# A gated attention-and-MLP block: score maxima of the first eight head pairs from key chunk differences, with a relu on ScalarE

## The chip, the cores and the metric

The kernel runs on one core of one Trainium2 chip. The metric is the device time of one execution in microseconds (us). The kernel before takes 1845.5 us, the median of three runs (1843.69 to 1846.99). Engines are named as the profile names them: PE (TensorE matmul), PEld (its weight load), DVE (VectorE), ACT (ScalarE), POOL (GpSimd), SP (SyncE, here only a DMA queue).

## The reference

Input x has S = 2048 rows and D = 640 columns; there are H = 32 heads of DH = 20 columns, and the token MLP has a hidden width of 1728. All is float32.

```
def _A_ref(x, wqkv, wo):
    qkv = (x @ wqkv).reshape(B, S, 3, H, Dh).transpose(2, 0, 3, 1, 4)
    q, k, v = qkv[0], qkv[1], qkv[2]
    scores = jnp.einsum("bhqd,bhkd->bhqk", q, k) * (Dh ** -0.5)
    p = softmax(scores, axis=-1)
    o = jnp.einsum("bhqk,bhkd->bhqd", p, v)
    return o.transpose(0, 2, 1, 3).reshape(B, S, D) @ wo

def _B_ref(x, w1, b1, w2, b2):
    h = layernorm(x, axis=-1)
    u = gelu(jnp.einsum("bsd,sf->bdf", h, w1) + b1)
    y = jnp.einsum("bdf,fs->bds", u, w2) + b2
    return y.transpose(0, 2, 1)

g = sigmoid((x * gate_w).sum(-1, keepdims=True))
return g * _A_ref(x, ...) + (1 - g) * _B_ref(x, ...)
```

## The kernel before

Float32 operands are split into a high and a low part (`hi_lo`: the high part by ACT or POOL, the difference by DVE or POOL), and a product is three matmuls. The work has four stages, one after the other on PE.

1. **Projections.** `qk_unit(m, w, q)` makes a 128x512 block of q (m below 5) or k (m from 5 on) in 15 matmuls; ACT writes the high part `evh`, DVE the low part `evl`, and SP stores both to `q_d` or `k_d`. `evh` and `evl` have two buffers each. Four quarters of x (`xh`, `xl`) are split by ACT and DVE as they arrive, between the first units. The v products and the layer norm's sums come between the second and the third block of q and k.
2. **The MLP** (`mlp`), a generator of 2592 steps; one step is a pair of 64-row matmuls of 320 columns (`pair64`). It has two column halves d; each makes 14 tiles u (48 steps, tail tile 32) and 16 tiles y (40 steps). ACT copies finished tiles out (`u_evac`, `y_evac`), POOL adds their two halves, ACT does the gelu and splits weights (`w_split`), POOL makes the weights' low parts. What must happen some steps later is put in the list `soon` with a countdown.
3. **The attention loop**: 16 head pairs, 32 iterations each, 512 in all. An iteration makes four transposed score tiles (`st`), ACT takes exp of each (`pt`), and PE multiplies the previous iteration's four exp tiles with v (`pv`).
4. **The output projection**, gate and store.

Softmax needs the row maxima ahead of the exp. They are made by a second stream of score tiles `s`, the generator `s_stream`: 16 pairs x 2 halves of the queries x 8 query tiles x 4 key chunks of 512 x 2 heads, 2048 tiles. Each is one PE matmul on 60 rows and one DVE `tensor_reduce` (L180) of 128x512 scores in PSUM to one column of `mx`. The two heads of a pair lie in PE's rows 0 to 63 and 64 to 127, so two neighbouring tiles of different heads run side by side. When a half is done, `s_max` and `s_store` reduce further, split and store to `m_d`, from which `load_m` puts the maxima into the extra rows of the q stack that `st` uses.

`s_next` takes the next tile of the stream. `S_AHEAD` = 736 tiles are taken in the MLP, two at a time and evenly over its steps; the other 1312 are taken in the loop, 2 or 3 in each of the first 484 iterations and none in the last 28. Where an engine's order is written by hand (all five engines, each from some point on) it is the order of the code. PSUM has eight banks: four for `st` and the MLP's tiles, three for `s`, one for `pv`. In the loop the third `st` of an iteration with two `s` tiles takes one of the `s` banks. The stacked operands of a pair, `ks` and `qs`, are loaded by 18 DMAs (`load_stack`); during the MLP they wait in the list `drip`, from which SP takes one every four `s` tiles.

Of the kernel before, what the change touches and what calls it, by code (L numbers as in the profile page):

```python
# [13 lines left out]
P = 128  # L14
# [5 lines left out]
FT = 14  # L20
TL = F - FF * P
# [7 lines left out]
def gated_mix(ctx, tc, xT, x, wqk, wv0, wv1, wo, w1, w1t, b1, w2, b2, out):  # L29
# [26 lines left out]
    k_d = dram.tile([2, D, S], F32, name="k_d")  # L56
    m_d = dram.tile([NP, 2, P, 32], F32, name="m_d")
# [13 lines left out]
    def s_tile(shape, name):  # L71
        return psum.tile(shape, F32, tag="s", bufs=3, name=name)
# [67 lines left out]
    def s_max(p, half, mx):  # L140
        mm = cp.tile([P, 16], F32, tag="mm", bufs=2, name=f"mm{p}_{half}")
        mc = cp.tile([P, 32], F32R, tag="mc", bufs=2, name=f"mc{p}_{half}")
        nc.vector.tensor_reduce(mm, mx.rearrange("p k j t -> p (j t) k"), axis=AX.X, op=OP.max)
# [24 lines left out]
    def s_tiles(p):  # L168
        for half in range(2):
            mx = cp.tile([P, 4, 2, 8], F32, tag="mx", bufs=2, name=f"mx{p}_{half}")  # L170
            for t in range(8):
                for kc in range(4):
                    for j in (1, 0):
                        def f(j=j, kc=kc, t=t):
                            ks, qs = s_src[p]
                            ps = s_tile([P, 512], f"s{p}_{half}_{t}_{j}_{kc}")
                            r = slice(64 * j, 64 * j + 3 * DH)
                            nc.tensor.matmul(ps, qs[half][r, t * P:(t + 1) * P], ks[r, kc * 512:(kc + 1) * 512],  # L178
                                             start=True, stop=True)
                            nc.vector.tensor_reduce(mx[:, kc, j, t: t + 1], ps, axis=AX.X, op=OP.max)  # L180
                        yield f
            s_close.append([2, lambda p=p, half=half, mx=mx: s_max(p, half, mx)])

    def s_stream(on_start):
        for p in range(NP):
            on_start(p)
            yield from s_tiles(p)
# [23 lines left out]
    accs = iter(range(1000))  # L211

    def qk_unit(m, w, q):
# [5 lines left out]
        hi_lo(hi, lo, ps, hi_eng=nc.scalar)  # L219
        dst = q_d if m < NC else k_d  # L220
# [3 lines left out]
        nc.sync.dma_start(dst[1, rows, cols], lo.bitcast(F32))  # L224

# [176 lines left out]
    for n, (m, q) in enumerate(units):  # L402
        if q == 0 and n + 4 < len(units):
            w[units[n + 4][0]] = load_w(units[n + 4][0])
        if n == 17:
            s_src[0] = base_stack(0, False, nc.gpsimd)
# [9 lines left out]
        qk_unit(m, w[m], q)  # L416
        if n in (18, 19):
            w_split(n - 18)
# [8 lines left out]

    soon = []
# [9 lines left out]
    def u_evac(f, d, ps, gh, gl):  # L438
# [4 lines left out]
        if f == FF:  # L443
            soon.append([7, lambda: u_swap(d, xg)])
            soon.append([30, lambda: nc.gpsimd.tensor_add(xg, xg, sws.pop())])
            soon.append([44, lambda: u_tail(f, d, xg, gh)])
        else:
            soon.append([18, lambda: u_gelu(f, xg, gh, gl)])
# [89 lines left out]
    S_AHEAD = 736  # L538
    STEPS = 2 * ((FT - 1) * 48 + 32 + NT * 40)

    def start_ahead(p):
        if 2 <= p + 1 < 6:
            s_src[p + 1] = base_stack(p + 1, False, None)
# [4 lines left out]
    for n, _ in enumerate(steps):  # L548
        settle()
        while done + 2 <= S_AHEAD and done < S_AHEAD * (n + 1) / STEPS:  # L550
# [7 lines left out]
            if drip and done % 4 == 0:  # L558
                drip.pop(0)()
# [27 lines left out]
    s_src[6] = s_stack(6)  # L587
# [83 lines left out]
    LEFT = NP * 128 - S_AHEAD  # L671
    for p in range(NP):
# [3 lines left out]
        for it in range(32):  # L676
# [121 lines left out]
```

## Time and profile before

| stage | us from the span's start | length | PE matmuls | ACT busy | DVE busy | POOL busy |
|---|---|---|---|---|---|---|
| projections | 0 to 225.3 | 225.3 | | | | |
| MLP with 736 maximum tiles | 225.3 to 698.5 | 473.2 | 5956 | 226.95 | 466.38 | 382.77 |
| loop, iterations with maximum tiles | 699.5 to 1707.5 | 1008.0 | 7112 | 987.11 | 852.42 | 181.26 |
| loop, last 28 iterations | 1707.5 to 1762.5 | 55.0 | 338 | 55.00 | 5.62 | 11.89 |
| output projection | 1762.5 to 1844.8 | 82.3 | | | | |

The span of the profiled execution is 1844.8 us, 0.7 us under the median of the runs (1845.5). No other time of that execution is given, and sums are made against 1844.8. Busy time is the time in which at least one instruction of the engine ran; PE's is no measure of its load, since its matmuls overlap and their ends are modelled. The granted clock of PE is 0.996 on average. The stages' bounds are the first and last matmuls and exps of the trace.

### The profile page before, as it was taken

To read this page: it belongs to the slowest core of one execution; us is meant where nothing else is said; L and a number is where in the kernel's file an instruction comes from. 1 tells how busy PE (TensorE), PEld (TensorE's weight loads), DVE (VectorE), ACT (ScalarE), POOL (GpSimd) and SP (SyncE) were. 2 spreads that over 40 slices of the span, in tenths; PEclk is the share of its full clock that TensorE was granted. 3 is DMA by queue.
4 is the path that set the end of the run, shared out by engine and by line. 5 is a ranking of instruction groups with operands and counts; after the bars stand their busy time and mean duration, and the time that the engine had idled before them with its cause. 6 is when DMAs were issued, how large, how long until landed. Compare 5 with 4: busy or idle time off the path is not lost. (4 is left out here: it accounts for less than half of the span.)

```text
span 1844.8 us, 39129 instructions
## 1 busy us (share of the span) xinstructions
PE 1829.7 (99%) x14978; PEld 1135.2 (62%) x14978; DVE 1428.9 (77%) x2341; ACT 1361.6 (74%) x2688; POOL 637.1 (35%) x900
## 2 busy tenths in 40 slices
PE   9999999999999999999999999999999999999998
PEld 7998799999999994333333333333333333333378
DVE  4202299999999998888888888888888888888137
ACT  4243244465444448999999999999999999999930
POOL 1013478888887770112112111121321211212210
PEclk9999999999999999999999999999999999999999
DMA  8456766566645645504032324213540423301463
GB/s 289 143 169 212 222 173 173 158 194 193 168 139 166 189 136 121 118 15 103 20 85 61 73 42 93 57 50 78 107 103 24 109 47 77 71 14 23 131 219 132
DMA packets 152831, 216.61 MB, mean 117 GB/s; under 512 B 65698, under 2 KB 92082, under 8 KB 148738
## 3 DMA queue, kind: packets, MB, share of 16 engines
q1 hardware_dynamic: 129172, 178.68, 35.4%
q0 software_dynamic: 14688, 20.78, 5.2%
q10 hardware_dynamic: 8784, 14.65, 2.4%
q8 instruction: 118, 1.93, 0.4%
q14 instruction: 69, 0.57, 0.1%
HBM read 165.43 MB, written 48.25 MB: 116 GB/s over the span
## 5 line engine op out<-in xcount | busy, mean ns | idle before, releaser
L180 DVE TENSOR_REDUCE mx<-s 128x1 f32<-128x512 f32 x2048 | 1293.7, 684 | 159.9 <-PE s L178 119.7
L703 ACT ACTIVATE p<-st 128x512 f32<-128x512 f32 x2048 | 1042.1, 615 | 20.9 <-PE s L178 2.2
L700 PEld LDWEIGHTS st<-qs_True,ks_True 62*128 62x128 f32 x2048 | 307.3, 185 | 485.1 <-ACT p L703 312.9
L700 PE MATMUL st<-qs_True,ks_True 62*128 62x512 f32 x2048 | 579.6, 425 | 0.2 <-ACT ty L477 0.2
L637 PE MATMUL pv<-p,v 128*32 128x512 f32 x4096 | 555.5, 605 | 0.2
L178 PE MATMUL s<-sk,sq 60*128 60x512 f32 x1280 | 423.1, 434 | 0.0
L41 POOL TENSOR_TENSOR wl<-wr,wh 128x512 fp32r<-128x512 f32 x228 | 273.6, 1216 | 59.8 <-ACT wh L38 30.9
L624 POOL DMA_DIRECT2D o_d<-oev x128 | 67.0, 524 | 494.3 <-DVE oev L618 491.6
L178 PE MATMUL s<-ks_False,qs_False 60*128 60x512 f32 x768 | 225.1, 397 | 0.4 <-DVE mx L180 0.3
L46 PE MATMUL y<-gh,wh 64*128 64x320 f32 x896 | 216.8, 308 | 0.0
L46 PE MATMUL y<-gl,wh 64*128 64x320 f32 x832 | 210.3, 306 | 0.0
L46 PE MATMUL y<-gh,wl 64*128 64x320 f32 x832 | 209.4, 305 | 0.0
L38 ACT ACTIVATE wh<-wr 128x512 fp32r<-128x512 f32 (+2 forms) x246 | 135.9, 594 | 90.2 <-PE s L178 29.0
L178 PEld LDWEIGHTS s<-sk,sq 60*128 60x128 f32 x1280 | 197.7, 185 | 1.2
L637 PEld LDWEIGHTS pv<-p,v 128*32 128x32 f32 x4096 | 84.9, 108 | 171.4 <-issue 156.4
L46 PE MATMUL u<-hl,wh 64*128 64x320 f32 x864 | 167.1, 306 | 0.0
L46 PE MATMUL u<-hh,wh 64*128 64x320 f32 x864 | 167.1, 306 | 0.0
L46 PE MATMUL u<-hh,wl 64*128 64x320 f32 x800 | 156.9, 306 | 0.4 <-POOL wl L41 0.4
L46 PEld LDWEIGHTS y<-gh,wh 64*128 64x128 f32 x896 | 155.3, 184 | 0.4
L46 PEld LDWEIGHTS y<-gh,wl 64*128 64x128 f32 x832 | 147.0, 184 | 0.3
L46 PEld LDWEIGHTS y<-gl,wh 64*128 64x128 f32 x832 | 146.9, 184 | 0.0
L178 PEld LDWEIGHTS s<-ks_False,qs_False 60*128 60x128 f32 x768 | 124.4, 184 | 1.1 <-DVE mx L180 1.1
(124 smaller groups left out, 1817.6 us busy)
## 6 DMA issues: line engine op xcount, KB each, us to landing
wr<-in_w_dram SPq DMA_DIRECT2D x196, 256.0 KB
ks_True<-k_d SPq DMA_DIRECT2D x96, 160.0 KB
qs_True<-q_d SPq DMA_DIRECT2D x192, 80.0 KB
sk<-k_d SPq DMA_DIRECT2D x60, 160.0 KB
sq<-q_d SPq DMA_DIRECT2D x120, 80.0 KB
v_d<-vt SPq DMA_DIRECT2D x32, 168.0 KB
v<-v_d SPq DMA_DIRECT2D x16, 336.0 KB
xr<-in_xT_dram SPq DMA_DIRECT2D x20, 256.0 KB
```

The costliest lines, as they stand in the source:

```text
L38: nc.scalar.activation(hi, src, AF.Copy)
L41: (lo_eng or nc.vector).tensor_sub(lo, src, hi.bitcast(F32))
L46: nc.tensor.matmul(ps[k], a[r], b[r], start=start, stop=stop)
L178: nc.tensor.matmul(ps, qs[half][r, t * P:(t + 1) * P], ks[r, kc * 512:(kc + 1) * 512], start=True, stop=True)
L180: nc.vector.tensor_reduce(mx[:, kc, j, t: t + 1], ps, axis=AX.X, op=OP.max)
L624: nc.gpsimd.dma_start(o_d[DH * h: DH * h + DH, cols], ev[r: r + DH, :])
L637: nc.tensor.matmul(pv[r: r + 32, :], v_tiles[p][:, kt, 10 * j: 10 * j + 32], pts[j, c], start=(kt == 0), stop=(kt == NT - 1))
L700: nc.tensor.matmul(ps, ks[r, kt * P:(kt + 1) * P], qs[qh][r, c * 512:(c + 1) * 512], start=True, stop=True)
L703: nc.scalar.activation(pt, ps, AF.Exp, scale=SCALE)
```

## The change

**Maxima.** For pairs 0 to 7 (`NDIFF`) the projections also store `kd_d`: for key chunks 0 and 2 the difference to the next chunk (`dh`, `kd`), for chunks 1 and 3 the keys themselves again. `load_stack` loads from it: for head 1 of a pair all four chunks, for head 0 the first two. A tile made with a difference is passed through relu by ACT into SBUF (`s_over`); the next chunk's tile is added to it and reduced to the maximum in one fused DVE call (`s_two`), since max(a, b) = b + relu(a - b). Of the eight tiles of a query tile, three go to ACT, three to the fused call and two to a plain reduce (`s_one`); before, eight went to a plain reduce. The fused call is two DVE instructions, one on 128x512 and one that writes a 128x1 result. Pairs 8 to 15 stay as they were (`s_raw`).

**Order.** In `s_diff` the head-0 fused tile is put off by one group (`late`). `S_AHEAD` is 1082 (1080 tiles and two empty steps) in place of 736, so the loop keeps 968 tiles and takes two in each of its first 484 iterations. In the MLP the tiles rotate over four banks (two `s`, one `s3`, the idle `pv` bank); in the loop `s` has two banks, and the third `st` of each iteration always takes `s3`.

**Around it.** The second half's layer norm (`h_norm` with d = 1) goes from two ACT instructions to one on DVE. The tail tile's countdowns in `soon` go from 30 and 44 to 70 and 100. Pair 0's stack is loaded through SP instead of POOL, and `drip` is emptied twice as fast.

```
+NDIFF = 8
+DROWS = 3 * 128
...
-            put(kf[r0: r0 + DH, :], k_d[0, rows, :])
-            put(kf[r0 + DH: r0 + 2 * DH, :], k_d[0, rows, :])
-            put(kf[r0 + 2 * DH: r0 + 3 * DH, :], k_d[1, rows, :])
+            cut = 0 if full or p >= NDIFF else S if j else S // 2
+            for n, lo in enumerate((0, 0, 1)):
+                r = slice(r0 + n * DH, r0 + (n + 1) * DH)
+                if cut:
+                    put(kf[r, :cut], kd_d[lo, rows, :cut])
+                if cut < S:
+                    put(kf[r, cut:], k_d[lo, rows, cut:])
...
+    def s_one(p, half, t, mx, j, kc, slot):
+        def f():
+            ps = s_mm(p, half, t, j, kc)
+            nc.vector.tensor_reduce(mx[:, slot, j, t: t + 1], ps, axis=AX.X, op=OP.max)
+        return f
+
+    def s_over(p, half, t, j, kc, over):
+        def f():
+            ps = s_mm(p, half, t, j, kc)
+            over[j, kc] = s_pool[0].tile([P, 512], F32, tag="over", bufs=3, name=f"ov{p}_{half}_{t}_{j}_{kc}")
+            nc.scalar.activation(over[j, kc], ps, AF.Relu)
+        return f
+
+    def s_two(p, half, t, mx, j, kc, slot, over):
+        def f():
+            ps = s_mm(p, half, t, j, kc)
+            ov = over.pop((j, kc - 1))
+            nc.vector.tensor_tensor_reduce(ov, ps, ov, 1.0, -3.0e38, OP.add, OP.max, mx[:, slot, j, t: t + 1])
+        return f
...
+                    yield s_over(*a, 1, 0, over)
+                    yield late
...
+                    yield s_over(*a, 1, 2, over)
+                    yield s_one(*a, mx, 0, 2, 1)
+                    yield s_two(*a, mx, 1, 1, 0, over)
+                    yield s_over(*a, 0, 0, over)
+                    yield s_two(*a, mx, 1, 3, 1, over)
+                    yield s_one(*a, mx, 0, 3, 2)
+                    late = s_two(*a, mx, 0, 1, 0, over)
...
+        nc.sync.dma_start(kd_d[0, rows, cols], hi.bitcast(F32))
+        nc.sync.dma_start(kd_d[1, rows, cols], lo.bitcast(F32))
+        kd = k_first.pop(c)
+        nc.vector.tensor_sub(kd, kd, ps)
+        dh = p1.tile([P, 512], F32R, tag="evh", bufs=2, name=f"dh{c}_{q}")
+        hi_lo(dh, kd.bitcast(F32R), kd, hi_eng=nc.scalar)
...
-        if d:
-            nc.scalar.activation(xm, xm, AF.Identity, bias=negm[:, t:t + 1])
-            nc.scalar.activation(xm, xm, AF.Copy, scale=rstd[:, t:t + 1])
-            return
-        nc.gpsimd.tensor_scalar(xm, xm, negm[:, t:t + 1], rstd[:, t:t + 1], op0=OP.add, op1=OP.mult)
+        (nc.vector if d else nc.gpsimd).tensor_scalar(xm, xm, negm[:, t:t + 1], rstd[:, t:t + 1], op0=OP.add, op1=OP.mult)
...
-        if n == 17:
-            s_src[0] = base_stack(0, False, nc.gpsimd)
+        if n == 8:
+            s_src[0] = base_stack(0, False, None)
...
-    S_AHEAD = 736
+    S_AHEAD = NDIFF * 128 + 2 + 56
...
-            due = min((p * 32 + it + 1) * LEFT // (NP * 32 - 28) + 1, LEFT)
-            take = min(due - given, 3)
+            take = min(LEFT - given, 2)
             for n in range(4):
-                st_op((n + turn) % 2, n // 2, s_tile if n == 2 and take < 3 else st_tile)
+                st_op((n + turn) % 2, n // 2, s3_tile if n == 2 else st_tile)
```

Three places show what this moves. The first is ACT's queue in the MLP's second half, about tile y 7: `ty` and `x` empty the two banks of a finished y tile, `wh` splits weights, and `ov` is the relu of a maximum tile. Before:

```order
L38 ACTIVATE wh_10723<-wr_10526 128x512
L477 ACTIVATE ty_7_10743<-y_7_0_10588,b2o,omg 128x320
L452 ACTIVATE x_10745<-y_7_1_10589,omg 128x320
L38 ACTIVATE wh_10751<-wr_10569 128x256
L38 ACTIVATE wh_10797<-wr_10590 128x512
L484 DMA y_d<-ty_7_10743 128x320
```

After, the same place:

```order
L206 ACTIVATE ov_0_6_0_0_12208<-s_0_6_0_0_12206 128x512
L565 ACTIVATE ty_7_12213<-y_7_0_12042,b2o,omg 128x320
L540 ACTIVATE x_12215<-y_7_1_12043,omg 128x320
L40 ACTIVATE wh_12221<-wr_12023 128x256
L206 ACTIVATE ov_0_7_1_0_12252<-s_0_7_1_0_12250 128x512
L40 ACTIVATE wh_12265<-wr_12044 128x512
L206 ACTIVATE ov_0_7_1_2_12275<-s_0_7_1_2_12273 128x512
L206 ACTIVATE ov_0_7_0_0_12295<-s_0_7_0_0_12293 128x512
L572 DMA y_d<-ty_7_12213 128x320
```

The relus now stand in ACT's queue behind the copies, splits and gelus of the MLP, and each of them holds an `s` bank until its turn.

The second place is PE in the loop, between two groups of `pv` matmuls. Before, an iteration with three maximum tiles:

```order
L700 MATMUL st_25_00_17640<-qs_True_16072,ks_True 128x512
L178 MATMUL s_1_2_1_3_17644<-sk_15338,sq_1_15340 128x512
L700 MATMUL st_25_10_17647<-qs_True_16072,ks_True 128x512
L178 MATMUL s_1_2_0_3_17651<-sk_15338,sq_1_15340 128x512
L700 MATMUL st_25_01_17654<-qs_True_16072,ks_True 128x512
L178 MATMUL s_1_3_1_0_17658<-sk_15338,sq_1_15340 128x512
L700 MATMUL st_25_11_17661<-qs_True_16072,ks_True 128x512
```

After, every iteration up to the 484th:

```order
L789 MATMUL st_31_00_19881<-qs_True_18267,ks_True 128x512
L193 MATMUL s_1_6_1_3_19885<-sk_16688,sq_1_16690 128x512
L789 MATMUL st_31_10_19888<-qs_True_18267,ks_True 128x512
L193 MATMUL s_1_6_0_3_19892<-sk_16688,sq_1_16690 128x512
L789 MATMUL st_31_01_19895<-qs_True_18267,ks_True 128x512
L789 MATMUL st_31_11_19899<-qs_True_18267,ks_True 128x512
```

The third maximum tile of 344 iterations has gone to the MLP.

The third place is ACT's queue in the projections, after the unit of k that ends the second quarter of x; `xh_3` is the last quarter's split. Before:

```order
L38 ACTIVATE evh_1_284<-qk_1_268 128x512
L38 ACTIVATE evh_1_306<-qk_1_290 128x512
L38 ACTIVATE xh_3_97<-xr_3_312 128x512
L38 ACTIVATE xh_3_101<-xr_3_316 128x512
L38 ACTIVATE xh_3_105<-xr_3_320 128x512
```

After:

```order
L40 ACTIVATE evh_1_287<-qk_1_271 128x512
L40 ACTIVATE evh_1_309<-qk_1_293 128x512
L40 ACTIVATE dh_1_318<-kf_0_249 128x512
L40 ACTIVATE xh_3_98<-xr_3_323 128x512
L40 ACTIVATE xh_3_102<-xr_3_327 128x512
```

The split `dh` of the difference stands ahead of the last quarter of x, and takes one of `evh`'s two buffers.

More of the change, by code (lines that the diff above doesn't have):

```diff
@@ L166, in s_finish, with s_mm @@
             s_close.pop(0)[1]()
-    def s_tiles(p):
+    s_count, s_wide, s_pool = [0], [True], [None]
+    def s_mm(p, half, t, j, kc):
+        ks, qs = s_src[p]
+        n = s_count[0] % 4
+        s_count[0] += 1
+        name = f"s{p}_{half}_{t}_{j}_{kc}"
+        if n < 2 or not s_wide[0]:
+            ps = s_tile([P, 512], name)
+        elif n == 2:
+            ps = s3_tile([P, 512], name)
+        else:
+            ps = psum.tile([P, 512], F32, tag="pv", bufs=1, name=name)
+        r = slice(64 * j, 64 * j + 3 * DH)
+        nc.tensor.matmul(ps, qs[half][r, t * P:(t + 1) * P], ks[r, kc * 512:(kc + 1) * 512], start=True, stop=True)
+        return ps
@@ L169, in s_tiles, with s_raw @@
+    def s_raw(p):
         for half in range(2):
-            mx = cp.tile([P, 4, 2, 8], F32, tag="mx", bufs=2, name=f"mx{p}_{half}")
+            mx = mx_tile(p, half)
             for t in range(8):
@@ L173, in s_tiles @@
                     for j in (1, 0):
[L174 to L182, printed above, removed]
+                        yield s_one(p, half, t, mx, j, kc, kc)
+            s_close.append([2, lambda p=p, half=half, mx=mx: s_max(
+                p, half, [mx[:, :, j].rearrange("p k t -> p t k") for j in range(2)])])
     def s_stream(on_start):
-        for p in range(NP):
+        yield from s_diff(on_start)
+        for p in range(NDIFF, NP):
             on_start(p)
-            yield from s_tiles(p)
+            yield from s_raw(p)
     hooks = [None]
@@ L416, in gated_mix @@
         qk_unit(m, w[m], q)
+        for _ in range(min(2, len(drip))):
+            drip.pop(0)()
         if n in (18, 19):
@@ L557, in gated_mix @@
                 drip.append(lambda: load_v(0))
-            if drip and done % 4 == 0:
+            if drip:
                 drip.pop(0)()
```

52 lines of the change are left out of this document (43 added, 9 removed).

## The prediction

> **What bounds the kernel now.** I read the busy shares in slices first, then a table by stage, then short timelines inside the two stages that change. The page's parts 1 and 2 (tenths of busy time in 40 slices):
>
> ```profile
> PE   9999999999999999999999999999999999999998
> DVE  4202299999999998888888888888888888888137
> ACT  4243244465444448999999999999999999999930
> ```
>
> PE's row says little, since its ends are modelled. DVE is full in slices 5 to 15, the MLP, where ACT is half idle; ACT is full from slice 16 on, the loop. The stretches (us, busy and instructions of PE, PEld, DVE, ACT, POOL, then PE clock, DMA share, GB/s) are the MLP, the 484 iterations with maximum tiles, and the last 28 without:
>
> ```profile
> 225.30:698.50 473.20, 472.39 (x5956) 468.61 (x5956) 466.38 (x760) 226.95 (x461) 382.77 (x394) 1.00 0.58 167
> 699.50:1707.50 1008.00, 1007.91 (x7112) 389.75 (x7110) 852.42 (x1390) 987.11 (x1937) 181.26 (x368) 1.00 0.31 68
> 1707.50:1762.50 55.00, 54.88 (x338) 16.38 (x338) 5.62 (x6) 55.00 (x113) 11.89 (x16) 1.00 0.34 110
> ```
>
> DVE is busy for 98.6% of the MLP, which invites the reading that DVE limits it. The timeline of the MLP's PE (start, length, instruction) says otherwise:
>
> ```profile
> 499.79 6.41 DVE L180 TENSOR_REDUCE mx<-s 128x1 f32<-128x512 f32 x10
> ...
> 500.40 0.43 PE L46 MATMUL u<-hh,wh 64*128 64x320 f32 x2
> ...
> 500.55 0.43 PE L46 MATMUL u<-hl,wh 64*128 64x320 f32 x2
> ...
> 501.28 0.52 PE L178 MATMUL s<-ks_False,qs_False 60*128 60x512 f32 x2
> ...
> 501.51 0.44 PE L46 MATMUL u<-hh,wh 64*128 64x320 f32 x2
> ...
> 502.55 0.52 PE L178 MATMUL s<-ks_False,qs_False 60*128 60x512 f32 x2
> ```
>
> A step starts 0.147 us after the one before, and a pair of maximum tiles takes 0.23 us (501.28 to 501.51). From one pair to the next, 1.27 us, PE has no gap: 0.23 and seven steps. The whole stage by these: 2592 steps x 0.1465 = 379.7, and 368 pairs x 0.23 = 84.6, together 464.3 of 473.2 us. PE bounds the MLP, with 9 us of losses; DVE is merely nearly as full.
>
> In the loop, PE and ACT around iterations of three and of two maximum tiles:
>
> ```profile
> 999.86 4.87 ACT L703 ACTIVATE p<-st 128x512 f32<-128x512 f32 x9
> 1000.00 0.49 PE L700 MATMUL st<-qs_True,ks_True 62*128 62x512 f32 x1
> 1000.00 0.72 PE L178 MATMUL s<-sk,sq 60*128 60x512 f32 x2
> ...
> 1000.57 1.89 DVE L180 TENSOR_REDUCE mx<-s 128x1 f32<-128x512 f32 x3 [0.23 <-PE s L178]
> ...
> 1002.13 0.49 PE L700 MATMUL st<-qs_True,ks_True 62*128 62x512 f32 x1
> ...
> 1004.10 0.49 PE L700 MATMUL st<-qs_True,ks_True 62*128 62x512 f32 x1
> ```
>
> The iteration with three tiles lasts 2.13 us, the one with two 1.97. The diff's formula gives 344 of the first and 140 of the second: 344 x 2.13 + 140 x 1.97 = 1008.5, the stretch's 1008.0. The last 28, without maxima, take 55.0/28 = 1.96 with ACT never idle. So two tiles cost the loop almost nothing beyond ACT's exps; the third costs 0.16 us.
>
> **The change, part by part.**
>
> *Loop.* All 484 iterations take two tiles. At 1.97 us that is 953.5, a gain of 54.5; at ACT's floor of 1.96, 59. I take -56. The bound on the other side: a two-tile iteration of today stands between three-tile ones, and from now on one bank serves each third `st`. If iterations lasted 2.05, halfway between two and three tiles, 992 us would be left and the gain would be 16.
>
> *MLP, PE.* It gets 1080 - 736 = 344 tiles, 172 pairs x 0.23 = +39.6. Nothing hides this: PE bounds the stage. The move alone is therefore worth -56 + 39.6 = -16.4; all other losses come out of that.
>
> *MLP, DVE.* The groups that price the new work (mean ns after the comma):
>
> ```profile
> L41 DVE TENSOR_TENSOR evl<-qk,evh 128x512 fp32r<-128x512 f32 x40 | 27.4, 690 | 78.1 <-ACT evh L38 62.6 <-DMA q_d<-evl 12.3 <-DMA k_d<-evl 3.1
> L315 DVE COPY gs<-v 128x2 f32<-128x2 f32 x16 | 2.5, 159 | 28.9 <-ACT vt L312 28.9
> L736 DVE SCALAR_TENSOR_TENSOR oy<-a,g_t,oy 128x320 f32<-128x320 f32 x32 | 16.2, 544 | 16.1 <-PE a L732 16.1
> 11.60 3.09 DVE L41 TENSOR_TENSOR xl<-xr,xh 128x512 fp32r<-128x512 f32 x5
> ```
>
> The fused call does not occur before. Its large part is nearest to a two-input instruction of 512 columns: 0.69 alone, (3.09 - 0.69)/4 = 0.60 from start to start in a row. Its small part is nearest to a two-column copy: 0.16 alone, and perhaps 0.06 in a row. Bounds: 0.66 and 0.85; I take 0.74, nearer the row that overlaps. A plain reduce is (1.89 - 0.68)/2 = 0.60 in a row (in the loop above). A group of eight tiles then costs DVE 2 x 0.60 + 3 x 0.74 = 3.42 us (3.18 to 3.75). PE needs for the same group 8 x 2592/1082 = 19.2 steps and four pairs: 2.81 + 0.92 = 3.73. DVE is at 92%, less than before, and PE stays the bound. `h_norm` adds 16 DVE instructions of 320 columns, under 0.6 us each by L736: hidden in that slack.
>
> [...] Reduces that last 0.68 start 0.60 apart, so consecutive instructions overlap by some 0.08. [...]
>
> *MLP, ACT.* A relu costs between 0.53, exps in a row ((4.87 - 0.62)/8), and 0.63, a weight split alone; taken 0.53. 384 relus are +204 us; 32 layer-norm instructions go (-18). ACT is busy 227 - 18 + 204 = 413 of some 540 us. On average this fits, but the queue is in order, and these rows of the MLP show what stands ahead of a relu:
>
> ```profile
> L38 ACT ACTIVATE wh<-wr 128x512 fp32r<-128x512 f32 x196 | 116.0, 625 | 65.2 <-PE s L178 29.0 <-POOL ty L481 18.1 <-DMA wr<-in_w_dram 11.9
> L477 ACT ACTIVATE ty<-y,b2o,omg 128x320 f32<-128x320 f32 x31 | 19.2, 619 | 58.9 <-PE y L46 47.3 <-PE s L178 11.6
> L38 ACT ACTIVATE wh<-wr 128x256 fp32r<-128x256 f32 x40 | 16.2, 409 | 0.0
> L452 ACT ACTIVATE x<-y,omg 128x320 f32<-128x320 f32 x31 | 16.1, 519 | 0.0
> L458 ACT ACTIVATE xg<-xg,b_t 128x320 f32<-128x320 f32 x26 | 14.7, 564 | 50.0 <-POOL xg L442 50.0
> L440 ACT ACTIVATE xg<-u 128x320 f32<-128x320 f32 x28 | 12.2, 434 | 53.7 <-PE u L46 53.7
> L452 ACT ACTIVATE x<-u 128x320 f32<-128x320 f32 x28 | 12.1, 431 | 0.0
> L38 ACT ACTIVATE hh<-xm 128x320 fp32r<-128x320 f32 x16 | 7.5, 468 | 0.1
> ```
>
> A bank comes round again after two pairs, 3.73/2 = 1.86 us. Of these, 0.57 pass from matmul to reader (1000.00 to 1000.57 above) and 0.53 for the relu, so a relu may wait about 0.76 before PE stalls. ACT's blocks are longer: `xg`, `x`, `wh` are some 1.4 us after each u tile; `ty`, `x`, `wh` 1.55 after each y tile, 2.0 in the first half with `hh`; and the gelu waits for POOL's sum, 50/26 = 1.9 us each, with all behind it. These waits cost nothing today, since nobody waits for ACT. A relu comes every 1.24 us, so on average it meets a block half a relu gap after its start: excess 2.0 - 0.62 - 0.76 = 0.6 for 16 y tiles, 1.55 - 1.38 = 0.2 for the other 16, near zero for the u copies, plus some 0.4 per u tile where POOL's wait (shorter then, PE being slower) and the gelu join. 10 + 3 + 11 = 24 us. Bounds: 0, if the four banks take all of it; 54, if every block stalls PE by all it exceeds 0.76 (32 x 1.25 + 26 x 0.55). I take +24 and leave the 9 us of other losses as they are.
>
> *Projections.* Here PE runs ahead of ACT, except at two places. The rows of ACT, SP, DVE and PE:
>
> ```profile
> 23.52 0.60 ACT L38 ACTIVATE evh<-qk 128x512 fp32r<-128x512 f32 x1 [2.90 <-PE qk L52]
> 24.02 1.66 ACT L38 ACTIVATE xh<-xr 128x512 fp32r<-128x512 f32 x3
> ...
> 39.04 1.31 ACT L38 ACTIVATE evh<-qk 128x512 fp32r<-128x512 f32 x2 [7.24 <-DMA q_d<-evh]
> 31.34 0.33 SPq L223 DMA_DIRECT2D q_d<-evh  x1
> 65.32 0.46 PE L52 MATMUL v<-wv,xh 128*128 128x322 f32 x2
> ...
> 66.01 0.47 ACT L38 ACTIVATE wv<-wvr 128x322 fp32r<-128x322 f32 x1
> ...
> 66.76 0.48 DVE L41 TENSOR_TENSOR wv<-wvr,wv 128x322 fp32r<-128x322 f32 x1
> ```
>
> A stored `evh` frees its buffer 7.7 us after issue (31.34 to 39.04). The new `dh` at 24 us needs such a buffer and holds up the last quarter of x behind it by up to 4 us; PE wants that quarter at about 30 (65.32 less ten units of 3.5 us) and the splits take some 4 us, so 0 to 2 are lost. At 65 the first v product uses the last `wv` the moment DVE has it; `dh`, a subtraction and a low part now come ahead of it, 0.53 + 2 x 0.60: about 2 late. 2 MB more of stores by the first six units fall on busy DMAs. I take +3, bounds 0 and 8.
>
> *Without a price.* Pair 0's stack leaves POOL for SP, 21 DMAs from unit 8 on, two a unit: loaded some 35 us before its first use, and PE is not waiting for POOL there. The faster drip (three more pairs, 21 DMAs each) stands on an SP queue and on DMA engines used 58%. Output projection: unchanged.
>
> **Sum:** -56 + 39.6 + 24 + 3 = +10.6, against the profiled execution's 1844.8: 1855 (its span is 0.7 under the median).
>
> **Rivals.**
> 1. *The banks absorb ACT's blocks*: only 4 of the 24 us are lost, 1835. For it: ACT averages 76%, and a PE that stalls lets ACT catch up. Against: the block after a y tile is longer than a bank can wait. It decides where the loss falls under 13 us; then the kernel is faster.
> [...]
> [...]
> 4. *The loop does not get to its floor*: 2.05 an iteration, +40 on the forecast, 1895.
>
> **Chances.** Forecast 0.46 (its own range 1842 to 1875), rival 1 0.34 (1824 to 1843), rival 2 0.10, rival 3 0.03, rival 4 0.07. 0.2% is 3.7 us, about what a measurement of this kernel can tell from no change: 1841.8 to 1849.2. Of the forecast 0.08 lie inside and 0.38 above; of rival 1 0.03 inside and 0.31 below; the rest is slower. Faster 0.31, same 0.11, slower 0.58. The range leaves out rivals 3 and 4 (0.10) and some 0.05 of rival 1 at its lower end: 1826 to 1890.
>
> **What would show it.** Iterations of 1.96 to 1.98 over the whole loop, which begins at about 766 instead of 699.5; in the MLP, waits of PE's `s` matmuls for the ACT relu, after the y copies and gelus above all; DVE clearly under 98% there; the fused parts between 0.66 and 0.85 from start to start. I would be wrong if PE hardly waits for ACT (rival 1), or waits for DVE instead (rivals 2 and 3), or if the relu's and the fused call's own times lie outside their bounds.

## The result, and the profile after

The changed kernel takes 1864.92 us, the median of four runs (1863.78 to 1865.84), against 1845.4 of the kernel before beside it: a ratio of 1.0107, with a 95% interval from 1.0092 to 1.0121. It is slower by 19.5 us; the forecast was 1855, slower by 9.5. The sign is right and the time lies in the stated range, but the loss is twice the forecast's.

The profiled execution spans 1862.6 us, 17.8 more than the 1844.8 before. Three stretches of it, the MLP, the loop's 484 iterations with maximum tiles, and the 28 without (columns as in the prediction: start and end, length, busy and instructions of PE, PEld, DVE, ACT, POOL, then PE clock, DMA share, GB/s):

```profile
226.50:773.20 546.70, 531.80 (x6299) 510.86 (x6299) 469.89 (x1144) 410.40 (x814) 394.19 (x415) 0.99 0.57 157
774.40:1723.20 948.80, 948.53 (x6768) 331.74 (x6766) 649.98 (x1053) 948.80 (x1938) 174.94 (x348) 1.00 0.30 66
1723.20:1778.90 55.70, 55.70 (x342) 15.99 (x342) 5.62 (x6) 55.18 (x113) 11.88 (x15) 1.00 0.33 108
```

An iteration lasts 948.80/484 = 1.960 us, and ACT is busy for all of it: the loop stands on its floor. DVE, busy for 98.6% of the MLP before, is now busy for 86% (469.89 of 546.70), and ACT for 75%. The two rows of the page's slices show both changes (tenths of busy time):

```profile
DVE  5303278898888888866666666666766666667137
ACT  4244378887788777599999999999999999999920
```

By stage, with the last matmul of each as its end (before, the last `pv` came at 1763.0, half a microsecond behind the stage's end in the first table):

| stage | before | after | difference | forecast |
|---|---|---|---|---|
| projections | 225.3 | 226.5 | +1.2 | +3 |
| MLP | 473.2 | 546.7 | +73.5 | +63.6 |
| loop with its lead-in | 1064.5 | 1005.7 | -58.8 | -56 |
| output projection | 81.8 | 83.7 | +1.9 | 0 |

The miss lies in the MLP. From the starts of PE's matmuls I took, for every pair of maximum tiles, the time to the next pair less 0.1465 us for each step between and 0.23 for the pair itself. What is left over, summed by stretch, is PE's loss. It rises from 6.1 to 40.3 us (a pair counts where it starts):

| stretch, us | before | after | what stands there after |
|---|---|---|---|
| to 240 | 1.6 | 7.1 | the stage's start |
| 240 to 300 | 1.2 | 5.3 | u tiles |
| 300 to 370 | 0.5 | 1.6 | u tiles |
| 370 to 500 | 1.2 | 7.9 | y tiles of the first half |
| 500 to 511 | 0.1 | 3.5 | one stop for the layer norm |
| 511 to 640 | 1.0 | 5.2 | u tiles of the second half |
| 640 to 741 | 0.5 | 2.9 | y tiles of the second half |
| from 741 | - | 6.7 | the 56 plain tiles, beside y tiles |

What PE waits for, and one wait of ACT, from the list of waits of the MLP after, 226.5 to 773.2 us (engine and line, what released it: us in total, times, longest):

```profile
PEld s L193 <- ACT ov L206: 17.5, 25, 3.6
PE s L193 <- ACT ov L206: 10.6, 12, 3.3
ACT xg L546 <- POOL xg L530: 9.1, 12, 1.9
PEld s L193 <- DVE mx L199: 7.8, 27, 0.4
PEld s L193 <- DVE mx L213: 3.4, 3, 2.8
PE s L193 <- DVE mx L213: 2.5, 1, 2.5
```

The relu (`ov`) is what PE waits for most, as forecast; a weight load and its matmul can wait for the same release (at 237.52 us, 3.60 and 3.33), so the two rows are not added. The gelu's wait for POOL fell from 50.0 to 9.1 us.

*The start.* PE, ACT and SP from 229 us on, rows of the timeline:

```profile
229.55 1.77 ACT L206 ACTIVATE ov<-s 128x512 f32<-128x512 f32 x3
236.35 0.63 ACT L40 ACTIVATE wh<-wr 128x512 fp32r<-128x512 f32 x1 [5.03 <-DMA wr<-in_w_dram]
...
233.88 0.31 PE L48 MATMUL u<-hl,wtmp 64*128 64x320 f32 x1
237.52 0.80 PE L193 MATMUL s<-ks_False,qs_False 60*128 60x512 f32 x2 [3.33 <-ACT ov L206]
...
233.06 1.28 SPq L459 DMA_DIRECT2D wr<-in_w_dram  x3
```

ACT waits 5.03 us for weights whose DMA was issued at 233.06; relus stand behind that wait, and PE stands for some 3.5 us, from 234.0 to 237.5. Before, SP issued the same weights at 230.72:

```profile
230.72 2.24 SPq L374 DMA_DIRECT2D wr<-in_w_dram  x5
```

The stop costs more than its own length. The MLP cut in three, with PE's granted clock third from the end:

```profile
226.50:236.00 9.50, 6.42 (x70) 5.81 (x69) 5.18 (x11) 2.85 (x6) 2.60 (x2) 1.00 0.67 216
236.00:243.00 7.00, 5.48 (x38) 5.20 (x40) 2.70 (x7) 3.74 (x7) 3.80 (x3) 0.51 0.89 272
243.00:773.20 530.20, 519.89 (x6195) 499.85 (x6194) 462.00 (x1126) 403.81 (x801) 387.80 (x410) 1.00 0.56 154
```

The clock is halved for some 7 us around the end of the stop, and nowhere else in the MLP. From 237.5 to 243 PE works at that clock, where a step takes 0.27 us (two from 238.11 to 238.64) instead of 0.147; about half of these 5.5 us, up to 2.7, is an estimate of what it loses by it.

*The layer norm.* DVE, POOL and ACT after, at 502 to 506:

```profile
502.12 1.15 DVE L430 TENSOR_SCALAR xm<-xm,negm,rstd 128x320 f32<-128x320 f32 x1
505.76 0.45 DVE L430 TENSOR_SCALAR xm<-xm,negm,rstd 128x320 f32<-128x320 f32 x1 [2.49 <-DMA xm<-in_x_dram]
...
501.79 1.30 POOL L43 TENSOR_TENSOR wl<-wr,wh 128x512 fp32r<-128x512 f32 x1 [0.72 <-DVE mx L199]
...
503.10 0.84 ACT L40 ACTIVATE hh<-xm 128x320 fp32r<-128x320 f32 x2
506.24 0.47 ACT L40 ACTIVATE hh<-xm 128x320 fp32r<-128x320 f32 x1 [2.31 <-DVE xm L430]
```

DVE waits 2.49 us for a piece of x, ACT's `hh` waits 2.31 for DVE, the tiles' readers stand behind both, and PE stops from 504.0 to 506.9. The move to DVE put a DMA's delay into the queue of an engine that PE needs.

*The plain tiles* at the end, from the list of waits of 741 to 773.2: 23 waits of up to 0.4 us.

```profile
PEld s L193 <- DVE mx L199: 6.1, 23, 0.4
```

*The prices* of the new work, from the groups of the MLP after (busy us, mean ns of one | idle time before), and three DVE rows of the timeline:

```profile
L213 DVE CUSTOM_DVE_ANT_0 ov<-s,ov 128x512 f32<-128x512 f32 x384 | 263.5, 687 | 60.2 <-PE s L193 54.0 <-PE y L48 0.3
L213 DVE DVE_READ_ACCUMULATOR2_ANT mx<- 128x1 f32 x384 | 31.8, 83 | 0.0
L430 DVE TENSOR_SCALAR xm<-xm,negm,rstd 128x320 f32<-128x320 f32 x16 | 14.2, 885 | 2.5 <-DMA xm<-in_x_dram 2.5
L206 ACT ACTIVATE ov<-s 128x512 f32<-128x512 f32 x384 | 224.9, 597 | 84.0 <-PE s L193 79.6 <-PE y L48 1.9 <-PE u L48 1.0
...
496.37 0.67 DVE L213 CUSTOM_DVE_ANT_0 ov<-s,ov 128x512 f32<-128x512 f32 x1
496.97 0.08 DVE L213 DVE_READ_ACCUMULATOR2_ANT mx<- 128x1 f32 x1
497.03 0.69 DVE L199 TENSOR_REDUCE mx<-s 128x1 f32<-128x512 f32 x1
```

In a row the fused call takes 497.03 - 496.37 = 0.66 from start to start, the lowest of the prediction's values. Its second part starts 0.60 after the first, which is 0.67 long, and the reduce 0.06 after the second, which is 0.08 long: in these rows each starts before the one ahead of it has ended.

### The profile page after: what moved, and what is told of

Read it like the earlier page. It is cut to its first block, busy times and chain, and to the rows that moved or that the text cites. A ratio compares the mean times of both kernels' runs of the same rounds, so it can differ in the third digit from the quotient of the medians.

```text
span 1862.6 us, 40444 instructions
## 1 busy us (share of the span) xinstructions
PE 1832.7 (98%) x14978; PEld 1121.4 (60%) x14978; DVE 1241.1 (67%) x2407; ACT 1510.6 (81%) x3046; POOL 632.2 (34%) x882
## 5 line engine op out<-in xcount | busy, mean ns | idle before, releaser
L199 DVE TENSOR_REDUCE mx<-s 128x1 f32<-128x512 f32 x1280 | 832.8, 686 | 303.8 <-PE st L789 165.1
L792 ACT ACTIVATE p<-st 128x512 f32<-128x512 f32 x2048 | 1004.0, 822 | 0.0
L789 PEld LDWEIGHTS st<-qs_True,ks_True 62*128 62x128 f32 x2048 | 245.9, 184 | 530.2 <-issue 426.8
L789 PE MATMUL st<-qs_True,ks_True 62*128 62x512 f32 x2048 | 508.9, 436 | 0.1
L193 PE MATMUL s<-ks_False,qs_False 60*128 60x512 f32 x1152 | 326.1, 407 | 15.0 <-ACT ov L206 10.6
L193 PE MATMUL s<-sk,sq 60*128 60x512 f32 x896 | 325.0, 442 | 0.0
L213 DVE CUSTOM_DVE_ANT_0 ov<-s,ov 128x512 f32<-128x512 f32 x384 | 263.5, 687 | 60.2 <-PE s L193 54.0
L206 ACT ACTIVATE ov<-s 128x512 f32<-128x512 f32 x384 | 224.9, 597 | 84.0 <-PE s L193 79.6
L193 PEld LDWEIGHTS s<-ks_False,qs_False 60*128 60x128 f32 x1152 | 171.2, 185 | 30.4 <-ACT ov L206 17.5
L726 PEld LDWEIGHTS pv<-p,v 128*32 128x32 f32 x4096 | 102.2, 108 | 125.9 <-issue 116.7
```

Source lines behind the costliest of these rows:

```text
L199: nc.vector.tensor_reduce(mx[:, slot, j, t: t + 1], ps, axis=AX.X, op=OP.max)
L206: nc.scalar.activation(over[j, kc], ps, AF.Relu)
L213: nc.vector.tensor_tensor_reduce(ov, ps, ov, 1.0, -3.0e38, OP.add, OP.max, mx[:, slot, j, t: t + 1])
L726: nc.tensor.matmul(pv[r: r + 32, :], v_tiles[p][:, kt, 10 * j: 10 * j + 32], pts[j, c], start=(kt == 0), stop=(kt == NT - 1))
L789: nc.tensor.matmul(ps, ks[r, kt * P:(kt + 1) * P], qs[qh][r, c * 512:(c + 1) * 512], start=True, stop=True)
L792: nc.scalar.activation(pt, ps, AF.Exp, scale=SCALE)
```

## The experiments

Ratios are to runs of the kernel before beside them. Theories that lay the loss on ACT carry an A in the expectations, the rival that lays it on DVE a D, and the one that lays it on PE's own work for the added tiles a P. Losses in the MLP are the left-over sum defined above (6.1 before, 40.3 after). The runs that keep the changed kernel's projections end them at 227.5 to 228.4 us in their profiles, the changed kernel's at 226.5: 1 to 2 us of each comparison with it lie in a stage that these edits do not touch.

**Without the relus.** Left out: the relu of 384 tiles; the fused call adds a constant zero tile, so the maxima of pairs 0 to 7 are not the reference's.

```
-            nc.scalar.activation(over[j, kc], ps, AF.Relu)
+            over[j, kc] = zero[0]
...
```

> The 384 relus are left out: the tiles made with key differences are still computed by PE, but nothing reads them, and the fused DVE call adds a constant tile of zeros, so the maxima of pairs 0 to 7 are not the reference's. PE and DVE do the same work as in the changed kernel. Theory A (relus wait in ACT's in-order queue, and PE waits for the banks that they hold): PE's waits for the relu, 25.3 us by the list of waits, go; the MLP falls from 546.7 to about 521 and the whole to about 1840. Rival D (DVE's fused calls set the pace): the MLP stays within 6 us of 546.7, the whole at 1859 to 1865. Rival P (PE's own cost of the added tiles is higher than 0.23 us a pair): no change either, 1862 to 1865.

Measured: 1848.51 us, 1.0015 [1.0005, 1.0025]. The MLP, its losses 25.8:

```profile
228.30:761.20 532.90, 524.25 (x6298) 515.93 (x6299) 464.38 (x1146) 212.70 (x431) 391.37 (x415) 0.99 0.60 161
```

The relus cost 17 us by the medians: the mechanism is there. But only 14.5 us of the losses went, where theory A had 25.3 (it added PE's and PEld's rows, which can be the same wait). The 25.8 that remain lie in three places: 7.1 up to 300 us, where PE still stands for some 3.4 us at the start; 7.4 at the layer norm, where DVE now waits 4.90 us for its x; and 6.5 at the plain tiles.

```profile
497.54 0.45 DVE L430 TENSOR_SCALAR xm<-xm,negm,rstd 128x320 f32<-128x320 f32 x1 [4.90 <-DMA xm<-in_x_dram]
```

At all other u and y tiles the loss is 4.9, against 3.2 before: without the relus PE keeps its pace there.

**All tiles by plain reduces**, order and banks as after (the key differences are made and not used).

```
-        yield from s_diff(on_start)
-        for p in range(NDIFF, NP):
+        for p in range(NP):
```

> The order and the banks of the changed kernel, 1080 tiles in the MLP and two an iteration in the loop, but every tile reduced plainly, without differences, relus or fused calls. If DVE at 0.61 us a reduce then sets the MLP's pace: eight tiles take 4.9 us instead of PE's 3.73, 135 groups 660 us, the whole about 1975. If PE stays the bound and DVE has slack after all: about 1840. The loop should stay at 1.96 us an iteration in both cases.

Measured: 1981.82, 1.0738 [1.0722, 1.0754]. The MLP, and its largest wait of PE:

```profile
228.20:889.40 661.20, 643.63 (x6298) 513.37 (x6299) 660.44 (x1144) 215.07 (x429) 389.69 (x415) 1.00 0.49 129
...
PEld s L193 <- DVE mx L199: 144.5, 517, 0.8
```

1080 reduces in 661.2 us are 0.61 each, and DVE is hardly ever idle (660.44 us busy): it sets this stage, as expected. With the loop at 1.96 an iteration here too, the move of 344 tiles needs the relus, which take three of eight tiles off DVE; their price belongs to the move.

**No maximum tile in the first 96 steps.**

```
-                done < S_AHEAD * (n + 1) / STEPS
+                done < S_AHEAD * (n + 1 - 96) / (STEPS - 96)
```

> The changed kernel, but no maximum tile in the MLP's first 96 steps (two u tiles); the tiles are spread over the rest. Theory A: the relus are no longer queued behind weight splits that wait for the first weight load (ACT waits 5.0 us there, PE loses 7.1 us before 240 us), so 5 to 7 us go, less 1 to 2 for a pace 4% denser: 1858 to 1861. Rivals D and P: PE's start is late by the weights alone, and a denser pace costs: 1865 to 1868.

Measured: 1870.3, 1.0131 [1.0114, 1.0148], 5 us slower than after, where theory A had 4 to 7 less. PE now waits for the weights itself, rows of its list of waits:

```profile
PEld u L48 <- ACT wh L40: 4.8, 1, 4.8
PE u L48 <- ACT wh L40: 4.6, 1, 4.6
```

So the loss at the start is not the relus' doing: the weights come late, and whoever stands first in line waits.

**The weight splits spread out**: one of each step's splits comes five steps later.

```
-        while len(w_got) < min(k + 4, len(w_list)):
+        while len(w_got) < min(k + 3, len(w_list)):
             w_split(len(w_got))
+        if k + 3 < len(w_list):
+            soon.append([5, lambda: w_split(k + 3) if len(w_got) == k + 3 else None])
```

> The changed kernel, but each weight split is issued five steps (0.7 us of PE time) after its block begins, so that it does not follow ACT's copies of a finished tile at once; a relu may come between. Theory A in the form of the prediction (blocks of 1.4 to 2.0 us on ACT outlast the 0.76 us that a bank can wait): the blocks shrink by 0.4 to 0.6 us, and 5 to 8 us of the stalls go: 1857 to 1860. If ACT's load as such is what counts, or DVE, nothing changes: 1863 to 1866.

Measured: 1875.36, 1.0160 [1.0145, 1.0175], 10 us slower than after, where a gain or no change was expected; PE's waits for the relu grow.

```profile
PEld s L193 <- ACT ov L206: 24.2, 34, 2.0
```

The longest wait shrinks from 3.6 to 2.0, their number grows from 25 to 34 and their sum from 17.5 to 24.2: breaking the blocks up in this way does not help.

**Nobody reads the tiles of pairs 0 to 7.** Left out: their relus, fused calls and reduces (maxima zero); PE makes all tiles as after.

```
-            nc.vector.tensor_reduce(mx[:, slot, j, t: t + 1], ps, ...)
...
-            nc.scalar.activation(over[j, kc], ps, AF.Relu)
...
-            nc.vector.tensor_tensor_reduce(ov, ps, ov, ...)
...
+                nc.vector.memset(mx, 0.0)
```

> The changed kernel, but nothing reads the maximum tiles of pairs 0 to 7: their relus, fused calls and reduces are left out and their maxima are zeros. PE still makes all 1080 tiles in the MLP. If PE alone prices the moved tiles (172 pairs at 0.23 us, and no more), the MLP lasts 504 us plus a few for its start, the whole about 1825. If the added matmuls themselves cost more, or the weights' way through ACT and POOL holds PE up in this stage, it lasts 515 or more, the whole 1835 or more.

Measured: 1839.51, 0.9964 [0.9950, 0.9977]; a gain of 6.6 us, 4.6 by the profiled spans. This run also holds the new projections, so the prediction's sum for it is -16.4 + 3 = -13.4.

```profile
228.10:751.10 523.00, 519.58 (x6298) 501.73 (x6299) 54.69 (x136) 212.34 (x431) 390.85 (x415) 1.00 0.61 164
```

The MLP takes 523.0, 49.8 more than before instead of 39.6. Its losses are 16.6: 5.8 up to 300 us (2.8 before), 6.4 at the plain tiles, which DVE still reads, and 4.4 at all the rest (3.3 before). So 10 us more of losses than before, and 2.8 more in the projections, are there with no relu and no fused call; away from the start and the plain tiles a pair costs hardly more than the 0.23 of the prediction.

**The layer norm back on ACT**, with two instructions as before.

```
+        if d:
+            nc.scalar.activation(xm, xm, AF.Identity, bias=negm[:, t:t + 1])
+            nc.scalar.activation(xm, xm, AF.Copy, scale=rstd[:, t:t + 1])
+            return
...
```

> The changed kernel with the second half's layer norm back on ACT, two instructions in place of DVE's one. Theory A2: on DVE the last norm waits 2.5 us for its x, with maximum tiles behind it on DVE and the split behind it on ACT, and PE loses 3.5 us at 504; on ACT the same wait would hold up the relus instead, and 18 us of ACT work come back into a stage of 135 us: 1866 to 1872. If ACT has room there, only the DVE loss goes: about 1861.

Measured: 1877.31, 1.0164 [1.0149, 1.0178], some 11 us slower than after; losses 51.9, of which 11.7 between 430 and 500 us, where the norms are (after: 5.3).

```profile
PEld s L193 <- ACT ov L206: 34.4, 30, 4.4
```

Two more ACT instructions in each of these y blocks (4.5 us each for the eight tiles from 430 to 500 us) cost more than DVE's delays: having moved them is worth those 11 us.

**The gelu later**, 36 steps behind its u tile instead of 18, so that POOL's sum is always there.

```
-            soon.append([18, lambda: u_gelu(f, xg, gh, gl)])
+            soon.append([36, lambda: u_gelu(f, xg, gh, gl)])
```

> The changed kernel with the gelu of a u tile 36 steps after its copy instead of 18, so that ACT does not wait for POOL's sum. Theory A: the relus behind the waiting gelu are what PE waits for in the u tiles (about 9 us from 240 to 300 and from 511 to 640); 4 to 6 us go: 1859 to 1861. If it is ACT's own work and not its wait, nothing changes: 1863 to 1866.

Measured: 1869.0, 1.0115 [1.0099, 1.0131]; the same as after (1.0107). The expected gain is missing, but the run does not settle why. ACT's wait for POOL's sum is gone from the list of waits (9.1 us after). In its place PE waits for the gelu's result at the first y tiles of both halves, a wait that the changed kernel does not have:

```profile
PE y L48 <- ACT gh L40: 2.4, 2, 1.3
```

The losses at u tiles away from the start hardly move (6.5 instead of 6.8), those at y tiles rise from 10.8 to 16.0.

**Relus without DVE's readers.** Left out: fused calls and reduces of pairs 0 to 7 (maxima zero); the relus stay.

```
-            nc.vector.tensor_reduce(mx[:, slot, j, t: t + 1], ps, ...)
...
-            nc.vector.tensor_tensor_reduce(ov, ps, ov, ...)
...
+                nc.vector.memset(mx, 0.0)
```

> The changed kernel with the relus, but without DVE's readers of the tiles of pairs 0 to 7: the fused calls and plain reduces are left out, and these maxima are zeros. Together with the run without relus (1.0015 times the kernel before), the run without any reader (0.9964) and the changed kernel (1.0107) it splits the stalls. If ACT's and DVE's shares add up, DVE's is 1.0015 - 0.9964 = 0.5%, 9 us, and this one takes about 1.0056 times before, 1856. If PE's stalls are all ACT's, it stays at 1862 or more; if DVE is what lets ACT's blocks through to PE, it falls under 1850.

Measured: 1868.54, 1.0124 [1.0108, 1.0139], no faster than after. The largest wait of PE in the MLP, and the layer norm's split in ACT's timeline:

```profile
PEld s L193 <- ACT ov L207: 24.1, 27, 3.2
...
508.72 0.47 ACT L40 ACTIVATE hh<-xm 128x320 fp32r<-128x320 f32 x1 [2.68 <-DVE xm L430]
```

With the two runs above this makes a square. No readers: -6.6 us; DVE's alone (the run without relus): +2.8; ACT's alone: +23; both: +19.5. The relus cost 17 us beside DVE's readers and 30 without them; DVE's readers cost 9 us without the relus and nothing beside them: the losses don't add, and ACT's are the ones that decide. PE's losses in the MLP by place show why (stretches between the same tiles in each run, named by their times in the changed kernel):

| stretch, us | before | no readers | DVE's alone | ACT's alone | both |
|---|---|---|---|---|---|
| to 300 | 2.8 | 5.8 | 7.1 | 13.8 | 12.4 |
| 300 to 370, u tiles | 0.5 | 1.0 | 1.0 | 1.5 | 1.6 |
| 370 to 500, y tiles | 1.2 | 0.7 | 1.4 | 7.0 | 7.9 |
| 500 to 511, layer norm | 0.1 | 0.1 | 7.4 | 4.9 | 3.5 |
| 511 to 640, u tiles | 1.0 | 2.0 | 1.7 | 5.6 | 5.2 |
| 640 to 741, y tiles | 0.5 | 0.7 | 0.8 | 2.9 | 2.9 |
| from 741, plain tiles | - | 6.4 | 6.5 | 6.4 | 6.7 |

At the u and y tiles PE loses time only where the relus are there. At the layer norm the late x stops PE once, through DVE's queue, or through ACT's, whose split waits for the norm (2.68 us in the row above); with both it is still one stop. That stop is 7.3 of the 9 us that DVE's readers cost alone.

**Three banks in the MLP instead of four.**

```
-        n = s_count[0] % 4
+        n = s_count[0] % 3
```

> The changed kernel with three banks for the maximum tiles in the MLP instead of four. A bank then comes round after 1.5 pairs, 1.4 us instead of 1.86, and a relu may wait 0.3 us instead of 0.76. Theory A: each block of ACT costs PE up to 0.46 us more, at 32 y tiles and 52 blocks of u tiles: 15 to 40 us more, 1880 to 1905. If the slack of the banks is not what PE's stalls hang on: under 1872.

Measured: 1932.55, 1.0468 [1.0451, 1.0485], 67 us slower than after and more than expected; losses 111.2. The waits of PE in the MLP:

```profile
PEld s L193 <- ACT ov L206: 42.9, 69, 2.9
PEld s L193 <- DVE mx L213: 40.2, 126, 4.5
PE s L193 <- ACT ov L206: 26.8, 37, 2.6
PE s L193 <- DVE mx L213: 8.0, 10, 4.2
```

A bank less makes PE wait for the fused call 126 times where it did 3 times (PEld's rows), and longer for the relu too. Without the fourth bank the change would have lost 87 us instead of 19.5.

**The kernel before with pair 0's stack on SP** (alone, from the change):

```
-        if n == 17:
-            s_src[0] = base_stack(0, False, nc.gpsimd)
+        if n == 8:
+            s_src[0] = base_stack(0, False, None)
...
+        for _ in range(min(2, len(drip))):
+            drip.pop(0)()
```

> The kernel before with one part of the change: pair 0's stack loaded through SP from the ninth unit on, two DMAs a unit, instead of 18 DMAs on POOL's queue. If POOL's issues held up the layer norm, ACT's split behind it for 14.1 us and so the unit's copies until PE stood still for 3.4 us at 213 us, that goes: about 1841. If those waits have another cause, or SP is too full: 1844 to 1847.

Measured: 1841.96, 0.9968 [0.9955, 0.9980]; the projections end at 219.7 instead of 225.3. What went is this, in the kernel before (POOL's and ACT's timeline):

```profile
199.17 0.56 POOL L105 DMA_DIRECT2D ks_False<-k_d  x1
...
212.94 0.50 POOL L115 DMA_DIRECT2D qs_False<-q_d  x1 [0.73 <-DMA ks_False<-k_d]
...
214.94 0.47 ACT L38 ACTIVATE hh<-xm 128x320 fp32r<-128x320 f32 x1 [14.13 <-POOL xm L345]
```

POOL issues 18 DMAs from 199.17 to 213.4, 0.50 to 0.56 us each and more where one waits for another DMA (up to 2.10); the layer norm behind them on POOL's queue comes late, ACT's `hh` waits 14.13 us for it, the evacuation of PE's tiles stands behind `hh`, and PE stops from 213.1 to 216.7. Right behind that stop PE's granted clock is 0.50 for 3.4 us (217.2 to 220.6), where a matmul of 512 columns comes every 0.43 us instead of every 0.23.

**The kernel before with the key differences**, made and stored as after, not used.

```
+            nc.vector.tensor_copy(k_first[c], ps)
...
+        nc.vector.tensor_sub(kd, kd, ps)
+        hi_lo(dh, kd.bitcast(F32R), kd, hi_eng=nc.scalar)
+        nc.sync.dma_start(kd_d[0, rows, cols], dh.bitcast(F32))
```

> The kernel before, plus the key differences of the projections, made and stored and not used. If the first v products wait for the difference's split ahead of the last wv (PE stands 4.7 us at 66 to 71 us in the changed kernel) and nothing gives it back: 1849 to 1852. If the later parts of the stage have slack that takes it up: 1845 to 1847.

Measured: 1858.6, 1.0071 [1.0059, 1.0084], 13 us slower than before, where 1852 was the most that was expected; the projections end at 234.9, 9.6 later. PE at the first v product in this run:

```profile
70.39 0.54 PE L53 MATMUL v<-wv,xh 128*128 128x322 f32 x1 [2.49 <-DVE wv L42]
...
72.66 1.41 PE L53 MATMUL v<-wv,xh 128*128 128x322 f32 x2 [1.46 <-ACT wv L39]
```

And the same place after, on PE, ACT and DVE:

```profile
68.40 0.42 PE L54 MATMUL v<-wv,xh 128*128 128x322 f32 x1 [1.96 <-DVE wv L43]
70.66 1.40 PE L54 MATMUL v<-wv,xh 128*128 128x322 f32 x2 [1.70 <-ACT wv L40]
...
69.62 0.63 ACT L40 ACTIVATE dh<-kf 128x512 fp32r<-128x512 f32 x1 [2.02 <-DVE kf L308]
...
67.25 0.69 DVE L303 COPY kf<-qk 128x512 f32<-128x512 f32 x1 [1.50 <-DMA kd_d<-kf]
70.89 0.49 DVE L43 TENSOR_TENSOR wv<-wvr,wv 128x322 fp32r<-128x322 f32 x1
```

The single buffer of `kf` is still being stored when the next copy wants it (1.50 us), `dh` waits for the subtraction behind it, and the last `wv` waits for both: two stops within 5 us, in which PE loses 4.7. Behind them the granted clock is 0.50 for 6.8 us (from 68.9 us after, from 70.5 here); half of that, up to 3.4 us, is an estimate of what PE loses besides. In the changed kernel the stack's move pays for a part of this: the differences cost 10 to 13 us, the stack gives 4 to 6 back, and the stop at 213 to 217 does not come back. The two do not add up exactly (+9.6 - 5.6 = +4 of the profiles against +1.2 to +3.1 in the runs that hold both): in this run, with the stack still on POOL, a stop of 3.7 us at 221 to 225 is followed by 6.8 us at half the clock, where before it was 3.4; the granted clock is 0.994 on average in this run, 0.996 before.

**The kernel before with the stack on SP and a fourth bank in the MLP**: of the first 736 tiles every fourth goes to the `pv` bank.

```
+                            if cnt[0] % 4 == 0 and cnt[0] <= 736:
+                                ps = psum.tile([P, 512], F32, tag="pv", bufs=1, name=nm)
```

> The kernel before with two parts of the change: pair 0's stack through SP, and the idle pv bank as a fourth bank for the maximum tiles in the MLP. The first alone gave 1842. If part of the 9 us by which the MLP exceeds PE's own work is a wait for three banks that DVE empties just in time: 1836 to 1840. If not: 1841 to 1843.

Measured: 1839.74, 0.9968 [0.9955, 0.9980]. This run and the one with the stack alone are each some 6 us (by the ratios) faster than the kernel before, and faster than the changed one. The fourth bank adds nothing that the two ratios can tell apart (losses 4.4 against 6.0).

## Why the prediction was half right

- **Loop, -56**: right, -58.8. Two tiles fit beside ACT's exps (1.960 an iteration, against 55.0/28 = 1.96 without maxima before), and by the same figures the fixed third bank costs nothing.
- **MLP, PE, +39.6**: right. 172 more pairs at 0.23; the stage's +73.5 are these and 34 of losses.
- **MLP, ACT, +24**: the mechanism was right, and the size a quarter too large. By the square's table the relus cost, beside DVE's readers, some 18 us up to 300 us and at the u and y tiles behind it. By the table of stretches, after less before, the u tiles lost 9.4 (4.1 + 1.1 + 4.2; forecast 11), the y tiles of the first half 6.7 (forecast 10) and of the second 2.4 (forecast 3): 18.5 in all.
- **"I take +24 and leave the 9 us of other losses as they are"**: the second half of this is the step that failed. The other losses, 6.1 us between the pairs before, do not stay as they are. The run without relus, where the +24 has no cause left, still loses 25.8: 4.3 more than before up to 300 us, 7.3 more at the layer norm and 6.5 at the plain tiles. In the changed kernel the late weights at the start cost 5.5 more than before, the stop for the layer norm 3.4 and the plain tiles 6.7, together 15.6, and none of them stands in the sum. The smaller ACT term (18.5 for 24) hides a part of this. The run in which nobody reads the tiles shows the same for the bare move: 4.6 to 6.6 us gained instead of 13.4, with 6.4 lost at the plain tiles and 3.0 more than before up to 300 us.
- **The 56 plain tiles**, never priced, could have been: PE wants such a pair every 4.8 x 0.1465 + 0.23 = 0.93 us, and DVE needs 2 x 0.60 = 1.20 by the prediction's own row. 28 pairs x 0.27 = 7.5; measured 6.7. "PE stays the bound" was worked out for groups with relus alone.
- **`h_norm` on DVE, "under 0.6 us each", hidden**: wrong in size, 0.885 on average, and not hidden once: it brings a DMA wait into DVE's queue. That the move helps all the same (11 us, by the run that undoes it) was foreseen only as -18 us of ACT's busy time.
- **The gelu's wait for POOL, part of the 11 us at u tiles**: not shown. The run with the later gelu takes this wait away and brings in another one.
- **Fused call, 0.74 of 0.66 to 0.85**: inside, at the lower bound (0.66). **Relu, 0.53 to 0.63**: inside, 0.597 on average; three in a row take 1.77 us.
- **Projections, +3**: the sum came near (+1.2) by luck, since two errors cancelled. The differences cost 10 to 13, above the upper bound of 8: at the last quarter of x nothing was lost (the first v product starts at 64.8, before at 65.3), but at the first v products 4.7 where about 2 was expected, and more behind them, where the clock is 0.50 for 6.8 us. The stack, "without a price" since "PE is not waiting for POOL there", gives 4 to 6: PE was waiting for POOL, through ACT. The row was there in the trace of before (14.13 us of ACT for POOL's `xm`), and the prediction looked only at PE's own releasers.
- **The rivals.** Banks that absorb the blocks (1835): refuted, the relus cost 17 us. PE waiting for DVE instead (rivals 2 and 3): refuted for the stage, DVE is busy for 86%, a fused call's large part takes 0.687 us for 512 columns, and both parts 0.66 from start to start; it holds for the 56 plain tiles. The range's upper end, 1890, would need dearer work on DVE, which no run of the changed kernel shows: 0.66 a fused call, where the forecast took 0.74. The loop off its floor (1895): refuted, 1.960 an iteration.

The granted clock of 0.99 in the MLP (1.00 before) comes from the stretch around the stop at its start: it is 0.51 from 236 to 243 us and 1.00 in all the rest. What stays open: why the weights come later at the start of the MLP, what ACT's wait for POOL's sum costs, and the 1.9 us of the output projection. No run separates these.

## What to carry to other kernels

When work moves to an engine whose queue is in order and already has blocks in it, price not its busy share but how long the slot that it holds (here a PSUM bank) can wait; four banks made this a loss of 1%, three make it 5%. Check each stretch of the stage separately, its start and its last tiles too, since a mean over the stage hides where another engine sets the pace. And before a step is written down as free because PE does not wait for its engine, follow the waits one engine further: here PE waited for ACT, and ACT 14.13 us for a queue of DMA issues on POOL.

## What the hardware showed that was not expected

- The second instruction of a fused call (`DVE_READ_ACCUMULATOR2_ANT` in the rows above) is 83 ns long, and the reduce behind it starts 0.06 us after it; the call itself is as long as a plain reduce (both 687 ns on average in the MLP, for 512 columns), so the second operand, from SBUF, adds nothing that these rows show.
- The layer norm on DVE (128x320, one input from SBUF) takes 0.44 or 0.45 us where none of POOL's subtractions `wl` has more than 0.05 us still to run, and up to 1.35 where one has: of 16, the 12 that began with 0.4 us or more of POOL's `wl` still to run took 0.66 to 1.35, the other four 0.44 or 0.45. At 502.12 above it ends at 503.27, 0.18 after POOL's (501.79 + 1.30 = 503.09), and so do all twelve (0.17 to 0.20 behind POOL): none ended before POOL did. What ties the two engines together there, no row shows.
- A DMA issue on POOL took 0.50 to 0.56 us of POOL's time before, and one that waited for another DMA (2.10 us at 205.28) stopped everything behind it: 18 of them held POOL's queue for 14.3 us.
- A stop of PE can cost more than its length. Behind the stop of 3.5 us at the MLP's start the granted clock is 0.51 from 236 to 243 us; behind the longer stop at the layer norm in the run without relus it is 0.50 for 6.8 us (497.2 to 504.0; the average of that run is 0.993, of the changed kernel 0.995). Behind the stop of 2.7 us at the same place in the changed kernel (504.2 to 506.9) it stays at 1.00. What decides between the two, these runs do not show.
